# Sliding-window attention and a rational MLP on one core: from two stages to one pipeline of 256-token steps

## The chip, the cores and the metric

The kernel runs on one core of one Trainium2 chip. The metric is the device time of one execution in microseconds (us). The kernel before was run three times: 406.58, 409.15 and 409.23 us, with a median of 409.15 us.

The engines are named as in the profile: PE is TensorE (matrix products; PEld is its loading of weights), DVE is VectorE, ACT is ScalarE, POOL is GpSimd, and SP is the engine that issues most of the DMAs here. Each engine works through its own queue of instructions in the order in which it was written.

## The reference

```python
def _attn_ref(q, k, v, n_sink, window):          # q, k, v: (4, 8, 768, 64); 4 sinks, window 128
    scores = scale * np.matmul(q, k.transpose(0, 1, 3, 2))
    is_sink = pos[None, :] < int(n_sink)
    rel = pos[:, None] - pos[None, :]
    in_window = (rel >= 0) & (rel < int(window))
    scores = np.where(is_sink | in_window, scores, -1000000000.0)
    a = np.exp(scores - max); a = a / (sum(a) + 1e-09)
    return np.matmul(a, v)

x = attn_out.transpose(0, 2, 1, 3).reshape(3072, 512)
h = x @ w_in                                     # w_in (512, 2048)
P = a[0] + a[1] * h + a[2] * h**2 + a[3] * h**3
Q = 1.0 + np.abs(b[0]) * np.abs(h) + np.abs(b[1]) * h**2
out = (P / (Q + 1e-6)) @ w_out                   # w_out (2048, 512)
```

Each of 32 heads (4 batches of 8) attends over 768 positions: a position sees the 127 before it, itself, and the first four positions. The heads of a token are then put side by side, and the 3072 rows of 512 go through an MLP whose activation is a quotient of two polynomials.

## The kernel before

The kernel has two stages, one after the other. A scheduler that knows the dependences lays out each engine's queue; the order of the calls in the program is its guide.

**Attention** works on 16 pairs of heads (`for p in range(NPAIR + 5)`, L294). For each pair `load` (L181) issues six float32 loads on SP (lines 188 to 194), in runs of 64 numbers. `prepare` (L198) casts q on DVE (L202) and k on ACT into a tile with zeros between the heads (L205), and turns both by DMA (L210, L212); `prepare_v` casts v on DVE (L223). K and V stand in blocks of 64 positions; in each, one head has the upper 64 partitions and the other the lower, so that one product serves two heads. `scores` (L239) makes four products of 128x192 (L245), takes the exponential on ACT (L249) and multiplies two triangles of each block with a mask on DVE (L255). `attend` (L260) adds up to five products of 128x130 (L276), the last of them for the sinks, and divides on DVE by the sum, which stands in a 65th column (L281, L282). `emit_x` (L288) turns the result by DMA into `xT`, which holds all tokens.

**MLP** works on 24 units, 6 blocks of 512 tokens by 4 quarters of the hidden size; a unit is a tile of 128x2048 in bfloat16. `project_in` (L345) makes 32 products of 128x512 and ACT copies them out (L349). On DVE come the square (L359; every fourth unit on ACT, L357), the magnitude by a bit mask (L360), the denominator's sum (L363), the two halves of the numerator (L365, L368, L370, L371). ACT makes the reciprocal as exp(-ln) (L376, L379). The last product (L408, called the gate below) multiplies the two, and `project_out` (L387) makes 16 products of 128x512 for each 128 tokens, which ACT copies out (L390).

The call order sets how far the units overlap: the gate of a unit is called after the next unit's whole numerator and denominator (L396 to L412).

## Time and profile before

| | |
|---|---|
| median of three runs | 409.15 us (406.58 to 409.23) |
| the profiled execution's own time | 405.44 us |
| its span in the trace | 403.7 us |
| mean granted clock of PE, share of full speed | 0.871 |
| busy, share of the span | DVE 65%, PE 61%, ACT 57%, POOL 10% |
| DMA traffic | 44.36 MB, of which 41.96 MB on SP's queue (q1) and 2.14 MB on POOL's (q0) |

The span is what the trace covers; the execution's own time is 1.7 us longer. Busy shares are averages over both stages. In a page's slices the span is cut into 40 equal parts of 10.1 us, and a digit gives the tenths of a slice that something was busy. In a timeline an instruction's duration overlaps a little with the next one's start on the same engine, so what an instruction costs in a full queue is the distance from start to start.

### The profile page before, as it was taken

The page shows a single profiled execution, that of the slowest core. Times are in us where ns is not written, and L with a number is a line of the kernel's source. Part 1 is how long each engine was busy: PE and PEld are TensorE (multiplying, and loading weights), DVE is VectorE, ACT ScalarE, POOL GpSimd, SP SyncE. Part 2 cuts the span into 40 slices and gives each one's busy share as a digit, 9 for nine tenths or more (in the row PEclk, how much of TensorE's full clock was granted, in tenths as well). Part 3 has the DMA queues.
Part 4 walks back from the last instruction along what each step waited for, and adds up shares of the span by engine and source line. Part 5 has one row for each costly group of instructions (what it writes and reads, how often), then busy time and mean ns, then how long its engine had stood idle before and what let it go on. Part 6 is the DMA issues. An engine that isn't in the chain of part 4 may idle for free.

```text
span 403.7 us, 4046 instructions
## 1 busy us (share of the span) xinstructions
PE 248.1 (61%) x1403; PEld 132.8 (33%) x1424; DVE 260.8 (65%) x404; ACT 228.7 (57%) x212; POOL 40.2 (10%) x89
## 2 busy tenths in 40 slices
PE   0000015473318442744797697999999999999666
PEld 0000013253207331633552243443443443444222
DVE  0035804292207330553669999999999999999950
ACT  1002216462426232542538978978978978978741
POOL 7504970000000000000000000000000000000000
PEclk9999999595657565575899989999999999999969
DMA  8999999989999999898430001001001001001102
GB/s 253 199 222 233 189 187 193 189 146 187 189 178 157 197 184 194 150 189 168 95 59 0 2 2 52 28 27 52 28 26 52 28 26 52 28 27 53 54 26 78
DMA packets 132629, 44.36 MB, mean 110 GB/s; under 512 B 126944, under 2 KB 129024, under 8 KB 132096
## 3 DMA queue, kind: packets, MB, share of 16 engines
q1 hardware_dynamic: 129984, 41.96, 57.0%
q0 software_dynamic: 2624, 2.14, 3.2%
q8 instruction: 11, 0.18, 0.2%
...
## 4 chain that ended last, share of the span: by engine, by line
DVE 44%; DMA 16%; PE 15%; SPq 10%; issue 6%; POOL 5%; ACT 4%; POOLq 0%; DVEq 0%; ACTq 0%
DMA kT<-k_bd 7%; DVE g_t L408 6%; DVE odd L370 6%; DVE num L371 6%; PE ps_o L276 6%; PE ps_out L387 5%; DVE s_sq L359 5%; DVE num L368 4%; DVE odd L365 4%; DMA q_in<-in_q_dram 4%; SPq L210 3%; DVE den L360 3%; DVE den L363 2%; SPq L188 2%; DVE x_n L282 2%
## 5 line engine op out<-in xcount | busy, mean ns | idle before, releaser
L387 PE MATMUL ps_out<-w_out_sb,g_t 128*128 128x512 bf16 x376 | 91.7, 388 | 17.2 <-DVE g_t L408 14.4
L345 PE MATMUL ps_h<-xT,w_in_sb 128*128 128x512 bf16 x376 | 89.9, 383 | 3.9 <-ACT hb L349 3.4
L245 PE MATMUL ps<-qT,kT 128*128 128x192 bf16 x192 | 32.5, 306 | 86.1 <-DMA kT<-k_bd 77.5
L205 ACT ACTIVATE k_bd<-k_in 64x768 bf16<-64x768 f32 x32 | 26.9, 841 | 71.3 <-DMA kT<-k_bd 56.9
L376 ACT ACTIVATE lnq<-den,one_eps,qsc 128x2048 f32<-128x2048 bf16 x24 | 50.3, 2096 | 20.3 <-DVE den L363 20.2
L387 PEld LDWEIGHTS <-g_t 128*128 128x128 bf16 x384 | 37.3, 100 | 68.3 <-DVE g_t L408 24.0
L249 ACT ACTIVATE e_bd<-ps 128x768 bf16<-128x768 f32 x48 | 37.2, 809 | 39.2 <-PE ps L245 23.1
L345 PEld LDWEIGHTS <-w_in_sb 128*128 128x128 bf16 x384 | 37.7, 98 | 50.7 <-issue 8.4
L349 ACT ACTIVATE hb<-ps_h 128x1024 bf16<-128x1024 f32 x48 | 48.6, 1013 | 6.7 <-PE ps_h L345 6.7
L245 PEld LDWEIGHTS <-kT 128*128 128x128 bf16 x192 | 21.9, 122 | 90.9 <-DMA kT<-k_bd 78.7
L276 PE MATMUL ps_o<-v_bd,e_bd 128*128 128x130 bf16 x352 | 39.5, 265 | 10.4 <-DVE x_n L282 6.3
L379 ACT ACTIVATE rden<-lnq 128x2048 bf16<-128x2048 f32 x24 | 45.7, 1903 | 0.0
L202 DVE CAST q_bf<-q_in 128x768 bf16<-128x768 f32 x16 | 11.7, 728 | 49.1 <-DMA qT<-q_bf 31.8
L276 PEld LDWEIGHTS <-e_bd 128*128 128x128 bf16 x352 | 30.8, 120 | 16.7 <-DVE x_n L282 8.9
L255 DVE TENSOR_TENSOR e_bd<-e_bd,edge 128x512 bf16<-128x512 bf16 x48 | 19.2, 413 | 21.3 <-ACT e_bd L249 21.3
L408 DVE TENSOR_TENSOR g_t<-num,rden 128x2048 bf16<-128x2048 bf16 x24 | 29.4, 1226 | 0.1
L371 DVE TENSOR_TENSOR num<-num,odd 128x2048 bf16<-128x2048 bf16 x24 | 29.4, 1226 | 0.0
L370 DVE TENSOR_TENSOR odd<-odd,hb 128x2048 bf16<-128x2048 bf16 x24 | 29.4, 1226 | 0.0
L363 DVE TENSOR_TENSOR den<-den,s_sq 128x2048 bf16<-128x2048 bf16 x24 | 29.4, 1226 | 0.0
L230 PE MATMUL ps<-qT,k_sink 128*128 128x128 bf16 (+1 forms) x27 | 7.8, 404 | 30.2 <-POOL k_sink L213 30.2
L359 DVE TENSOR_TENSOR s_sq<-hb 128x2048 bf16<-128x2048 bf16 x18 | 22.1, 1226 | 3.3 <-ACT hb L349 3.3
L223 DVE CAST v_bd<-v_in 64x768 bf16<-64x768 f32 x32 | 20.0, 624 | 5.8 <-PE ps_o L276 3.9
...
## 6 DMA issues: line engine op xcount, KB each, us to landing
...
out_dram<-o_t SPq DMA_DIRECT2D x24, 256.0 KB, 2.0
...
qT<-q_bf SPq DMA_TRANSPOSE x16, 4.9
kT<-k_bd SPq DMA_TRANSPOSE x16, 3.8
```

Of the source, the lines that this page charges most:

```text
L245: nc.tensor.matmul(ps[:, n // 2, (n % 2) * 192:(n % 2) * 192 + 192], lhsT=kT[:, j, :], rhs=qT[:, 64 * j:64 * j + 192], start=True, stop=True)
L276: nc.tensor.matmul(ps_o[:, n, :], lhsT=l_, rhs=r_.rearrange("p e c -> p (e c)"), start=(m == 0), stop=(m == len(terms) - 1))
L345: nc.tensor.matmul(ps_h[:, j, :], lhsT=w_in_sb[c][:, fc * P:(fc + 1) * P], rhs=xT[c][:, t0:t0 + TB], start=(c == 0), stop=(c == NDMC - 1))
L349: nc.scalar.activation(out=hb[:, half * 2 * TB:(half + 1) * 2 * TB], in_=ps_h, func=AF.Copy)
L359: nc.vector.tensor_tensor(out=s_sq, in0=hb, in1=hb, op=ALU.mult)
L363: nc.vector.tensor_tensor(out=den, in0=den, in1=s_sq, op=ALU.add)
L370: nc.vector.tensor_tensor(out=odd, in0=odd, in1=hb, op=ALU.mult)
L371: nc.vector.tensor_tensor(out=num, in0=num, in1=odd, op=ALU.add)
L376: nc.scalar.activation(out=lnq, in_=den, func=AF.Ln, scale=qsc, bias=one_eps)
L379: nc.scalar.activation(out=rden, in_=lnq, func=AF.Exp, scale=-1.0)
L387: nc.tensor.matmul(ps_out, lhsT=g_t[:, co:co + P], rhs=w_out_sb[fc], start=(fc == 0), stop=(fc == NFFC - 1))
L408: nc.vector.tensor_tensor(out=g_t, in0=pend[2], in1=rden, op=ALU.mult)
```

## The change

Both stages become one loop over 12 steps of 256 tokens (three per batch, all eight heads). A step has two half-steps for the attention (two pairs of heads each) and two units for the MLP, each half of the hidden size (128x2048 in bfloat16, as before). In turn i of the loop the MLP works on unit i, while the attention's scores stand three half-steps and its `attend` two half-steps ahead. `project_in` now makes 32 products of 128x256 for a unit; `project_out` makes 16 of 128x512 in each turn.

- q, k and v are loaded by POOL's queue, which casts to bfloat16 on the way: a q tile of 128 tokens and all heads in one DMA, k the same, v one DMA per head and step. The casts on DVE and ACT are gone.
- K is no longer turned by DMA: eight transposes on PE for a step, and two copies from PSUM on DVE put it into the block form. q and x are turned by DMA as before, in smaller pieces.
- E and V are held by step, E in two buffers and V in three.
- In PSUM, `ps_h` has two buffers of two banks, `ps_s` one of two banks, and one pool `ps_m` of two banks serves K's transposes, the sinks, `attend` and `project_out`.
- The square is made on ACT in every second unit instead of every fourth.

```diff
@@ -30,24 +30,90 @@
...
+    TS = 256
...
+    ps_hp = ctx.enter_context(tc.tile_pool(name="ps_h", bufs=2, space=bass.MemoryType.PSUM))
+    ps_sp = ctx.enter_context(tc.tile_pool(name="ps_s", bufs=1, space=bass.MemoryType.PSUM))
+    ps_mp = ctx.enter_context(tc.tile_pool(name="ps_m", bufs=2, space=bass.MemoryType.PSUM))
...
+    def load_q(tile_i):
+        b, T = divmod(tile_i, S // P)
+        t_ = a_kv.tile([P, H, D], BF16, tag="q_bf", name="q_bf", bufs=3)
+        nc.gpsimd.dma_start(out=t_, in_=q[b, :, T * P:(T + 1) * P, :].rearrange("h p d -> p h d"))
...
+        for t in range(NTS):
+            r0 = g * TS + t * P
+            nc.gpsimd.dma_start(out=t_[:, t, :].rearrange("p (h d) -> p h d", h=H),
+                                in_=k[b, :, r0:r0 + P, :].rearrange("h p d -> p h d"))
...
+        for h in range(H):
+            i, e = divmod(h, 2)
+            nc.gpsimd.dma_start(
+                out=t_[e * 64:(e + 1) * 64, i, :, e, 0:D],
+                in_=v[b, h, g * TS:(g + 1) * TS, :].rearrange("(j p) d -> p j d", p=64))
...
-        def load(p):
...
-            q_bf = a_q.tile([P, NT, P], BF16, tag="q_bf")
-            nc.vector.tensor_copy(out=q_bf, in_=q_in.rearrange("p t e d -> p t (e d)"))
-            k_n = k_nat2[p % 2]
-            for e in range(2):
-                nc.scalar.activation(out=k_n[e * 64:(e + 1) * 64, :, e * D:(e + 1) * D],
-                                     in_=k_in[e * 64:(e + 1) * 64], func=AF.Copy)
...
-            nc.sync.dma_start_transpose(out=qT[:, 0:NT, :],
-                                        in_=q_bf.rearrange("p t c -> p (t c)"))
-            nc.sync.dma_start_transpose(out=kT, in_=k_n.rearrange("p j c -> p (j c)"))
...
-            for e in range(2):
-                nc.vector.tensor_copy(out=v_n[e * 64:(e + 1) * 64, :, e, 0:D],
-                                      in_=v_in[e * 64:(e + 1) * 64])
...
+    def turn_q(tile_i):
...
+        nc.sync.dma_start_transpose(out=qT_fix[b % 2][:, :, T * P:(T + 1) * P],
+                                    in_=q_bf.pop(tile_i).rearrange("p h d -> p (h d)"))
...
+    def turn_k(s):
+        b, g = divmod(s, GPB)
+        ps = ps_mp.tile([P, 512], FP32, tag="ps_m", name="ps_kT").bitcast(BF16)
+        ps = ps.rearrange("p (i c) -> p i c", i=NPB)
+        kb = k_bf.pop(s)
+        for t in range(NTS):
+            for i in range(NPB):
+                nc.tensor.transpose(ps[:, i, t * P:(t + 1) * P],
+                                    kb[:, t, i * P:(i + 1) * P], ident)
+        kT = kT_fix[s % 2]
+        for e in range(2):
+            lo, hi = e * 64, (e + 1) * 64
+            nc.vector.tensor_copy(out=kT[lo:hi, :, lo:hi],
+                                  in_=ps[lo:hi].rearrange("p i (j c) -> p (i j) c", c=64))
...
-        for p in range(NPAIR + 5):
...
-            if i % 4 == 3:
-                nc.scalar.activation(out=s_sq, in_=hb, func=AF.Square)
...
+        ps_h = ps_hp.tile([P, UC // 2, TS], FP32, tag="ps_h", name="ps_h")
+        for n in range(UC // 2):
+            fc = u * UC + half * (UC // 2) + n
+            for c in range(NDMC):
+                nc.tensor.matmul(ps_h[:, n, :], lhsT=w_in_sb[c][:, fc * P:(fc + 1) * P],
+                                 rhs=xblk[m][:, c, :], start=(c == 0), stop=(c == NDMC - 1))
...
+    def scores(s, i):
+        b, g = divmod(s, GPB)
+        grp, il = divmod(i, 2)
+        e_t = e_fix[grp, s % 2]
+        ps = ps_sp.tile([P, 2, 512], FP32, tag="ps_s", name="ps_s")
+        for n in range(NHF):
+            c = g * TS + 64 * n
+            nc.tensor.matmul(ps[:, n // 2, (n % 2) * 192:(n % 2) * 192 + 192],
+                             lhsT=kT_fix[s % 2][:, i * NHF + n, :],
+                             rhs=qT_fix[b % 2][:, i, c:c + 192], start=True, stop=True)
+        data = e_t[:, 64:].rearrange("p (j c) -> p j c", c=EW)[:, il * NHF:(il + 1) * NHF, 0:192]
+        nc.scalar.activation(out=data.rearrange("p (a n) c -> p a n c", a=2),
+                             in_=ps[:, :, 0:384].rearrange("p a (n c) -> p a n c", n=2),
+                             func=AF.Exp, scale=inv_sqrt_d)
+
+    def mask(s, grp):
+        e_t = e_fix[grp, s % 2]
+        blocks = e_t[:, 64:].rearrange("p (j m c) -> p j m c", m=2, c=P)[:, :, :, 0:64]
+        nc.vector.tensor_tensor(
+            out=blocks, in0=blocks,
+            in1=edge0 if s % GPB == 0 else edge.unsqueeze(1).to_broadcast([P, 2 * NHF, 2, 64]),
+            op=ALU.mult)
...
+    def attend(s, i):
+        b, g = divmod(s, GPB)
+        grp, il = divmod(i, 2)
+        ps = ps_mp.tile([P, 512], FP32, tag="ps_m", name="ps_o")
...
+            for m, (l_, r_) in enumerate(terms):
+                nc.tensor.matmul(ps_o[:, n, :], lhsT=l_, rhs=r_.rearrange("p e c -> p (e c)"),
+                                 start=(m == 0), stop=(m == len(terms) - 1))
...
+        nc.vector.reciprocal(out=rec, in_=o4[:, :, D:D + 1])
...
+    def turn_x(s, grp):
+        if grp == 0:
+            xblk[s] = xpool.tile([P, NDMC, TS], BF16, tag="xblk", name="xblk")
+        for n in range(NTS):
             nc.sync.dma_start_transpose(
...
+        if i % 2 == 0:
+            nc.scalar.activation(out=sq[i], in_=hb[i], func=AF.Square)
+        else:
+            nc.vector.tensor_tensor(out=sq[i], in0=hb[i], in1=hb[i], op=ALU.mult)
...
+    def magnitude(i):
+        den[i] = m_sb.tile([P, UW], BF16, tag="den", name="den")
+        nc.vector.tensor_scalar(out=den[i].bitcast(U32), in0=hb[i].bitcast(U32),
+                                scalar1=0x7FFF7FFF, scalar2=None, op0=ALU.bitwise_and)
+
+    def denominator(i):
+        nc.vector.tensor_tensor(out=den[i], in0=den[i], in1=sq[i], op=ALU.add)
+
+    def even(i):
+        num[i] = m_sb.tile([P, UW], BF16, tag="num", name="num")
+        nc.vector.tensor_scalar(out=num[i], in0=sq[i], scalar1=a2, scalar2=a0,
+                                op0=ALU.mult, op1=ALU.add)
+
+    def odd(i):
+        nc.vector.tensor_scalar(out=sq[i], in0=sq[i], scalar1=a3, scalar2=a1,
+                                op0=ALU.mult, op1=ALU.add)
+
+    def odd_h(i):
+        nc.vector.tensor_tensor(out=sq[i], in0=sq[i], in1=hb[i], op=ALU.mult)
+
+    def numerator(i):
+        nc.vector.tensor_tensor(out=num[i], in0=num[i], in1=sq[i], op=ALU.add)
+
+    def log_den(i):
+        lnq[i] = m_sb.tile([P, UW], FP32, tag="lnq", name="lnq", bufs=1)
+        nc.scalar.activation(out=lnq[i], in_=den[i], func=AF.Ln, scale=qsc, bias=one_eps)
+
+    def recip_den(i):
+        with nc.allow_low_precision(reason="exp(-ln(q)) reciprocal, tol 2e-2"):
+            nc.scalar.activation(out=den[i], in_=lnq[i], func=AF.Exp, scale=-1.0)
+
+    def gate(i):
+        m, u = divmod(i, 2)
+        g_of[m, u] = g_sb.tile([P, UW], BF16, tag=f"g_{u}", name=f"g_{u}")
+        nc.vector.tensor_tensor(out=g_of[m, u], in0=num[i], in1=den[i], op=ALU.mult)
+
+    def project_out(m, tt, part):
+        if part == 0:
+            ps_out[m, tt] = ps_mp.tile([P, DM], FP32, tag="ps_m", name="ps_out")
+        for fc in range(part * UC, (part + 1) * UC):
+            u, fl = divmod(fc, UC)
+            co = fl * TS + tt * P
+            nc.tensor.matmul(ps_out[m, tt], lhsT=g_of[m, u][:, co:co + P], rhs=w_out_sb[fc],
+                             start=(fc == 0), stop=(fc == NFFC - 1))
+        if part == 1:
+            o_t = o_sb.tile([P, DM], FP32, tag="o_t", name="o_t")
+            nc.scalar.activation(out=o_t, in_=ps_out[m, tt], func=AF.Copy)
+            row0 = m * TS + tt * P
...
+    load_w_in(0)
+    feed(1)
+    load_v_sink()
+    load_w_in(1)
+    load_w_out()
+    for n in range(3):
+        turn_q(n)
+    turn_k(0)
+    for i in range(-3, NU + 4):
+        s_q, grp_q = divmod(i + 3, 2)
+        s_a, grp_a = divmod(i + 2, 2)
+        has_q = s_q < NSTEP
+        has_a = 0 <= s_a < NSTEP
+        has_m = 0 <= i < NU
+        back = i - 3
+        has_o = 0 <= back < NU
+        if has_q and grp_q == 0 and s_q + 2 < NSTEP:
+            feed(s_q + 2)
+        if has_q:
+            scores(s_q, 2 * grp_q)
+        if 0 <= i - 1 < NU:
+            log_den(i - 1)
+            even(i - 1)
+            odd(i - 1)
+        if has_m:
+            project_in(i, 0)
+        if has_a:
+            attend(s_a, 2 * grp_a)
+        if 0 <= i - 1 < NU:
+            odd_h(i - 1)
+        if has_q:
+            scores(s_q, 2 * grp_q + 1)
+        if 0 <= i - 1 < NU:
+            recip_den(i - 1)
+        if has_m:
+            project_in(i, 1)
+        if has_a:
+            attend(s_a, 2 * grp_a + 1)
+            turn_x(s_a, grp_a)
+        if has_q and grp_q == 0 and 1 <= s_q + 1 < NSTEP:
+            load_v(s_q + 1)
+        if 0 <= i - 1 < NU:
+            numerator(i - 1)
+        if has_q:
+            mask(s_q, grp_q)
+        if has_m:
+            magnitude(i)
+            square(i)
+            denominator(i)
+        if has_o:
+            project_out(back // 2, back % 2, 0)
+        if has_q and grp_q == 0:
+            sink_scores(s_q)
+        if has_q and grp_q == 1 and s_q + 1 < NSTEP:
+            for n in (2 * s_q + 3, 2 * s_q + 4):
+                if n < NQT:
+                    turn_q(n)
+            turn_k(s_q + 1)
+        if 0 <= i - 1 < NU:
+            gate(i - 1)
+        if has_o:
+            project_out(back // 2, back % 2, 1)
```

What the change moves is seen in the engines' queues. First DVE in the middle of the MLP, before; `g_t` is the gate, and `den` is first the magnitude and then the denominator's sum:

```order
L359 TENSOR_TENSOR s_sq<-hb 128x2048
L360 TENSOR_SCALAR den<-hb 128x1024
L365 TENSOR_SCALAR odd<-s_sq,acoef 128x2048
L363 TENSOR_TENSOR den<-den,s_sq 128x2048
L368 TENSOR_SCALAR num<-s_sq,acoef 128x2048
L370 TENSOR_TENSOR odd<-odd,hb 128x2048
L408 TENSOR_TENSOR g_t<-num,rden 128x2048
L371 TENSOR_TENSOR num<-num,odd 128x2048
```
DVE now, in the middle of the loop, for one even unit; `kT` is K in block form, `ps_kT` its transposes, `e` the exponentials, `g` the gate:

```order
L237 COPY kT_181<-ps_kT 64x16x64 x2
L358 TENSOR_TENSOR den<-den,sq 128x2048
L362 TENSOR_SCALAR num<-sq,acoef 128x2048
L366 TENSOR_SCALAR sq<-sq,acoef 128x2048
L311 RECIPROCAL rec<-ps_o 128x4
L370 TENSOR_TENSOR sq<-sq,hb 128x2048
L313 TENSOR_TENSOR x_n<-ps_o,rec 128x2x128
L373 TENSOR_TENSOR num<-num,sq 128x2048
L311 RECIPROCAL rec<-ps_o 128x4
L281 TENSOR_TENSOR e_1_173<-e_1_173,edge 128x16x64
L313 TENSOR_TENSOR x_n<-ps_o,rec 128x2x128
L388 TENSOR_TENSOR g_2978<-num,den 128x2048
```
Before, the gate in this piece is that of the preceding unit: the sum `den<-den,s_sq` of the next unit stands ahead of it. Now the gate, the last row, follows its own unit's numerator, and the next unit's magnitude, K's copies (or a square) and sum all stand behind it; the magnitude of the unit shown is the row ahead of the first.

ACT before, for one unit and the start of the next; `lnq` and `rden` are the reciprocal's two halves, `hb` the copies of `project_in`, `o_t` the copy of `project_out`:

```order
L357 ACTIVATE s_sq<-hb 128x2048
L376 ACTIVATE lnq<-den,one_eps,qsc 128x2048
L349 ACTIVATE hb<-ps_h 128x1024
L379 ACTIVATE rden<-lnq 128x2048
L349 ACTIVATE hb<-ps_h 128x1024
L390 ACTIVATE o_t<-ps_out 128x512
```
ACT now, for the unit whose rows of DVE stand above; `den<-lnq` is the reciprocal's second half:

```order
L383 ACTIVATE den<-lnq 128x2048
L342 ACTIVATE hb<-ps_h 128x1024
L348 ACTIVATE sq<-hb 128x2048
L402 ACTIVATE o_t<-ps_out 128x512
L274 ACTIVATE e_1_173<-ps_s 128x4x192
L379 ACTIVATE lnq<-den,one_eps,qsc 128x2048
L342 ACTIVATE hb<-ps_h 128x1024
L274 ACTIVATE e_1_173<-ps_s 128x4x192
L383 ACTIVATE den<-lnq 128x2048
L342 ACTIVATE hb<-ps_h 128x1024
```
Between the two halves of the reciprocal there now stands an exponential of the attention besides the one copy of `project_in`. A second exponential stands ahead of the first half.

POOL at the start of the program, now:

```order
L72 MEMSET v_bd_92 128x2080
L72 MEMSET v_bd_96 128x2080
L74 MEMSET v_bd_92 64x16 x2
L72 MEMSET v_bd_100 128x2080
L74 MEMSET v_bd_96 64x16 x2
L80 DMA q_bf<-in_q_dram 128x8x64
L74 MEMSET v_bd_100 64x16 x2
L80 DMA q_bf<-in_q_dram 128x8x64 x2
L88 DMA k_bf<-in_k_dram 128x8x64 x2
L97 DMA v_bd_92<-in_v_dram 64x4x64 x8
masks.py:197 MEMSET ident 128x128
L117 MEMSET edge 128x128
```
Before PE can turn K it needs `ident`, which POOL fills after three fills of V's buffers and 13 loads; before, POOL's queue began with the mask and the loads of `w_out`.

## Rows read from the trace of the kernel before

**Rows 1.** The page, engines: busy us (share of the span) and instructions.
```profile
PE 248.1 (61%) x1403; PEld 132.8 (33%) x1424; DVE 260.8 (65%) x404; ACT 228.7 (57%) x212; POOL 40.2 (10%) x89
```

**Rows 2.** The page, DMA in 40 slices: mean busy share of 16 engines, in tenths.
```profile
DMA  8999999989999999898430001001001001001102
```

**Rows 3.** Stretches: length, busy us (count) PE PEld DVE ACT POOL, clock, DMA, GB/s.
```profile
100.00:120.00 20.00, 5.52 (x33) 3.92 (x32) 4.01 (x10) 5.81 (x8) 0.88 (x5) 0.59 1.18 182
220.00:240.00 20.00, 15.63 (x64) 6.46 (x64) 20.00 (x22) 18.83 (x13) 0.00 (x0) 0.91 0.00 1
340.00:360.00 20.00, 19.44 (x87) 8.49 (x88) 20.00 (x21) 19.10 (x15) 0.00 (x0) 1.00 0.07 27
```

**Rows 4.** The page, DMA queues: packets, MB, share of 16 engines' span.
```profile
q1 hardware_dynamic: 129984, 41.96, 57.0%
q0 software_dynamic: 2624, 2.14, 3.2%
```

**Rows 5.** Timeline in the MLP, VectorE and ACT: start us, us, instruction.
```profile
217.62 0.68 DVE L360 TENSOR_SCALAR den<-hb 128x1024 uint32<-128x1024 uint32 x1
218.22 0.80 DVE L365 TENSOR_SCALAR odd<-s_sq,acoef 128x2048 bf16<-128x2048 bf16 x1
218.95 1.21 DVE L363 TENSOR_TENSOR den<-den,s_sq 128x2048 bf16<-128x2048 bf16 x1
220.08 0.80 DVE L368 TENSOR_SCALAR num<-s_sq,acoef 128x2048 bf16<-128x2048 bf16 x1
220.20 2.09 ACT L376 ACTIVATE lnq<-den,one_eps,qsc 128x2048 f32<-128x2048 bf16 x1 [0.87 <-DVE den L363]
```

**Rows 6.** Groups of instructions on ACT: busy us, mean ns | idle before.
```profile
L349 ACT ACTIVATE hb<-ps_h 128x1024 bf16<-128x1024 f32 x48 | 48.6, 1013 | 6.7 <-PE ps_h L345 6.7
L379 ACT ACTIVATE rden<-lnq 128x2048 bf16<-128x2048 f32 x24 | 45.7, 1903 | 0.0
...
L249 ACT ACTIVATE e_bd<-ps 128x768 bf16<-128x768 f32 x48 | 37.2, 809 | 39.2 <-PE ps L245 23.1 <-PE ps_o L276 15.8
...
L390 ACT ACTIVATE o_t<-ps_out 128x512 f32<-128x512 f32 x24 | 14.4, 599 | 10.7 <-PE ps_out L387 10.7
```

**Rows 7.** Groups on VectorE in the attention, columns as in 6.
```profile
L255 DVE TENSOR_TENSOR e_bd<-e_bd,edge 128x512 bf16<-128x512 bf16 x48 | 19.2, 413 | 21.3 <-ACT e_bd L249 21.3
L282 DVE TENSOR_TENSOR x_n<-ps_o,rec 128x256 bf16<-128x256 f32 x48 | 19.2, 417 | 6.9 <-DMA xT<-x_n 6.4
...
L281 DVE RECIPROCAL rec<-ps_o 128x4 f32<-128x4 f32 x48 | 8.3, 176 | 4.1 <-PE ps_o L276 3.4
```

**Rows 8.** Timeline, VectorE: one cast of V.
```profile
200.40 0.56 DVE L223 CAST v_bd<-v_in 64x768 bf16<-64x768 f32 x1
```

**Rows 9.** Chain of waits, TensorE at full clock: start us, us, what, times.
```profile
204.67 1.27 PE ps_o L276 x20
...
366.24 3.45 PE ps_h L345 x16
```

**Rows 10.** Groups on POOL, columns as in 6.
```profile
L84 POOL DMA_DIRECT2D w_out_sb<-in_moe_w_out_dram x16 | 8.8, 553 | 3.9 <-DMA w_out_sb<-in_moe_w_out_dram 3.3 <-issue 0.5
...
L155 POOL MEMSET v_bd<- 128x1560 bf16 x3 | 5.0, 1680 | 0.1
L172 POOL DMA_DIRECT2D v_sink_f<-in_v_dram x8 | 4.6, 579 | 0.0
```

**Rows 11.** DMA issues: KB of each, median us from issue to landing.
```profile
out_dram<-o_t SPq DMA_DIRECT2D x24, 256.0 KB, 2.0
...
xT<-x_n SPq DMA_TRANSPOSE x16, 2.9
```

**Rows 12.** Timeline, POOL and VectorE, at 46 us.
```profile
46.08 3.10 POOL L162 MEMSET e_bd<- 128x3136 bf16 x1
...
46.55 3.03 DVE L202 CAST q_bf<-q_in 128x768 bf16<-128x768 f32 x1
```

**Rows 13.** Chain of waits, TensorE in the attention, columns as in 9.
```profile
121.99 2.02 PE ps_o L276 x17
```

450 lines of the change are left out of this document (164 added, 286 removed).

## The prediction

> **What bounds the kernel now.** The page's first part comes first: no engine is busy for more than 65% of the span [rows 1], so the span must hold stages with different limits. The slices show them: the DMA engines are 80 to 100% busy for the first 19 of 40 slices and nearly idle after [rows 2]. A table of stretches then gives each stage's limit [rows 3]. In the attention, 100 to 120 us, TensorE, VectorE and ACT are busy for 5.5, 4.0 and 5.8 of 20 us while the DMA engines are full: the transfers bound it. In the MLP, 340 to 360 us, VectorE is busy for 20.0 of 20 us, TensorE for 19.4 and ACT for 19.1. The attention with its start takes about 206 us (its last products end at 205.9 us [rows 9]), the MLP the other 198. In the transfers, q1's 129,984 packets take 57% of 16 engines' span [rows 4]: 0.57 x 403.7 x 16 / 129,984 = 28 ns each.
>
> **What goes, comes and moves.** Three costs have to be found: one turn of the new loop, the start before the first unit, and the end after the last. The attention's transfers, which bound the first stage, drop to 73,728 packets of q, k and v (18.9 MB in runs of 256 bytes) and half of the 49,152 packets of the transposes (12.6 MB, of which K with its zeros was half): at 28 ns that is 98,304 x 28 / 16 = 172 us, spread over the whole span, so no longer the bound. That casting packets cost the same no row shows. The nearest above are the 2,624 of q0, mostly of 1 KB: 0.032 x 403.7 x 16 / 2,624 = 79 ns, or 364 us for the 73,728; I take 28, because size sets most of it, and keep the other end for a rival.
>
> The turn. Its work on each engine, from start-to-start distances in the full queue [rows 5]: a two-input product or sum of 128x2048 costs VectorE 1.13 us, a polynomial's half 0.73, the magnitude 0.60.
> - VectorE: 4.5 of the first (the square only in every second unit), 2 halves, 1 magnitude, or 7.1 us; two divisions with their reciprocals, 2 x 0.59 = 1.2 [rows 7]; one mask of 128x1024, between the 0.41 of half its size and 0.83, say 0.7; K's copies, one pair in two turns. A copy of 64x1024 from PSUM is not in the trace. Below it lies the V cast, 0.56 us for 768 numbers [rows 8], or 0.75 for 1024; above it the division, which reads PSUM too: (417 - 176) / 252 = 0.96 ns per number over the reciprocal's four [rows 7], or 1.15 us. Neither row is nearer (one has the operation, the other the memory), so I take 0.95. In all 7.1 + 1.2 + 0.7 + 0.95 = 10.0 us.
> - ACT: Ln 2.09 [rows 5], Exp 1.90, two copies 2.02, two exponentials 1.62, output 0.60 [rows 6], half a square 0.95 (as Exp, which has its size), sinks about 0.2: 9.4 us.
> - TensorE at full clock: 1.27 / 20 = 64 ns for a product of 130 columns with its weights, 3.45 / 16 = 216 ns for 512 [rows 9]. So 32 of 256 at 108, 16 of 512 at 216, 18 of 130 at 64, 8 of 192 at 94, and some 6 small: 9.2 us.
>
> Three engines thus have nearly the same load, and order decides. The queues close a circle through two of them: sum on VectorE, Ln, copy, exponential and Exp on ACT, then gate, next magnitude, K's copies or square, next sum on VectorE. Before, the gate stood a half unit later and nothing waited for it. An odd unit's circle is 2.09 + 1.01 + 0.81 + 1.90 + 1.13 + 0.60 + 1.13 + 1.21 = 9.9, with two handoffs of 0.04 (sum done at 220.16, Ln at 220.20 [rows 5]) 10.0 us. In an even one the square is ACT's (1.01 + 1.90 = 2.9 us behind Exp, covered by 1.13 + 0.60 + 1.90) and K's two copies take its place: 10.75, with the bounds of the copy 10.35 to 11.15. The mean is 10.4 (10.2 to 10.6). [...] No row here shows a copy out of PSUM on VectorE.
>
> I add 0.2 for what waits at the change of step: x's last division is followed by two transposes that land 2.9 us after issue [rows 11], while TensorE has 16 x 0.216 = 3.5 us of output work and some K work as cover; with issue and queue it comes up to 1 us short in every second turn, and TensorE has slack for some of that. So 10.6 us a turn.
>
> The start. POOL fills three V buffers (1.68 us for 1560 columns [rows 10], so 2.2 each, 6.7), then issues 13 loads at 0.55 [rows 10] before `ident`: about 17 us with the small fills. K's turn and copies, then four rounds of scores and exponential in one PSUM buffer (about 1.6 us each): 27 us. But the divisions of step 0 stand on VectorE behind the eighth `w_in` cast, for which 4.2 MB of `w_in` and some 2.9 MB of loads must come: at the 182 GB/s of the attention's transfers [rows 3] 39 us, less with `w_in`'s longer rows: I take 37. Division, turning and landing: first unit at 41 us (33 if only the chain counts, 50 if `w_out` shares the transfers). Its 32 products at half clock (6.9), copy, square on ACT and sum: 11 us to the first Ln.
>
> The end. After the last Ln: 2.1 + 1.9 + gate 1.2 + 16 products 3.5 + output copy 0.6 + 2.0 to land [rows 11] = 11.3 us.
>
> **The sum.** 41 + 11 + 23 x 10.6 - 3 (the last turns have no exponentials and no K) + 11.3 = 304 us of span, against 403.7. The profiled execution took 1.7 us more than its span, 405.44, and the median of the runs 409.15 is 0.9% above it: 304 + 1.7 = 306, and 308 for a median. The casts on VectorE and ACT that go are counted for nothing of their own: they lay under the transfers [rows 2]. What is late next is VectorE, at 10.0 of 10.6 us.
>
> **Rivals.**
> - The circle has slack I don't see and transfers start sooner: VectorE's work alone, 9.7 with a quick copy, from 33 us: 33 + 11 + 223 - 3 + 11 = 275, a median of 280. For it: before, VectorE never waited in the MLP [rows 3]. Against: the order of the rows.
> - POOL's issues get in VectorE's way. A cast that takes about 0.56 us alone took 3.03 beside a POOL fill of 3.10 us [rows 12, 8]. In the MLP before, POOL did nothing [rows 3]; now it issues six loads a turn. If each of the three single-input operations of a unit met one issue of 0.55 [rows 10], a turn would be 10.4 + 1.7 = 12.1 us and the median 343. Against: rows of an issue beside VectorE there are none; in the fills POOL writes 128 partitions all the time. [...] Other small waits (two `ps_m` buffers for four uses) would end in the same place.
> - The loads bound. An issue of 128 rows takes 0.55 us, one of 16 rows 0.58 [rows 10], so rows seem free; a q or k tile has 1,024 runs. If they were not, 8 x 0.55 = 4.4 for 48 tiles, 1.1 for 96 V loads and 20 for the rest make 337 us of issuing, with five turns behind the last 390, a median of 395. It decides from 21 us of issuing per step, which two turns hide. With 79 ns a packet it ends near there too.
> [...]
>
> That the stages might not overlap is excluded: the queues interleave them.
>
> **Chances.** The forecast 0.57, the quick case 0.12, VectorE's waits 0.20, the loads 0.04, the clock 0.05, nothing that can be told 0.02. About 1% is what a measurement of this kernel can tell. Faster by over 1%: 0.93; within 1%: 0.02; slower: 0.05. The range reaches into the quick case (start at 33 us alone gives 300, with 9.8 a turn 281) and past the third (343): 282 to 352. Left out are the loads, the clock and the outer halves of the two others.
>
> **What would show it.** First `ps_h` product near 41 us; gates of successive units 10.0 and 10.75 us apart in turn; VectorE waiting up to a microsecond for ACT ahead of each gate, and nowhere else; a kT copy near 0.95 us; TensorE at full clock from there on; POOL's issues under 1 us for 1,024 runs. Wrong would be: gates 12 us or more apart, single-input operations of VectorE longer than before, TensorE waiting for x or `ps_m` longer than 1 us a turn, K's or Q's tiles late.

## The result, and the profile after

The changed kernel takes 320.06 us (median of 4 runs, 318.43 to 320.73) against 408.33 us (the kernel before, now with a fourth run): a ratio of 0.784, 95% interval 0.779 to 0.788. The profiled execution has a span of 318.6 us. The forecast was 308, from a sum of 304 us of span, so the sum was 14.6 us short, and its terms missed by more than that, in both directions.

First the page of the changed kernel: its engines, the granted clock and the DMA engines in 40 slices, and the two DMA queues (packets, MB, share of 16 engines).

```profile
PE 240.5 (75%) x1920; PEld 167.4 (53%) x1920; DVE 250.4 (79%) x384; ACT 212.8 (67%) x194; POOL 127.1 (40%) x192
...
PEclk9999556979858998999999999999999999999999
DMA  4999999999999996996960627549510111110011
...
q0 software_dynamic: 78976, 11.56, 58.1%
q1 hardware_dynamic: 31776, 16.79, 23.6%
```

Before, the busiest engine had 65% of the span [rows 1] and the DMA engines were full for the first half and idle in the second [rows 2]. Now VectorE has 79%. The transfers did not spread over the span, though: the DMA engines are full from 8 to about 120 us, thin out up to 225 us, where the last load is issued, and are then nearly idle. A packet of q0 took 0.581 x 318.6 x 16 / 78,976 = 37.5 ns, where the forecast took 28 and had 79 as its other end. (The DMA share adds up the times of all packets and can pass 1, as the 1.60 from 48 to 112 us in the next table does.)

The table of stretches of the changed kernel, as [rows 3] before (us, busy us of each engine and its instructions, granted clock, DMA share, GB/s):

```profile
48.00:112.00 64.00, 45.50 (x372) 33.46 (x372) 41.61 (x67) 38.50 (x34) 45.85 (x63) 0.82 1.60 118
112.00:225.00 113.00, 101.30 (x857) 71.04 (x855) 105.52 (x156) 95.24 (x88) 44.32 (x63) 0.98 0.76 77
225.00:300.00 75.00, 69.34 (x563) 48.48 (x562) 68.74 (x93) 63.26 (x57) 0.00 (x0) 1.00 0.15 42
```

From 48 to 112 us, with the transfers full, TensorE, VectorE and ACT are busy for 71, 65 and 60% of the time. From 112 us on they have 90, 93 and 84%. So the new pipeline has a slow first third and an even rest. Where one ends is read from ACT's Ln, one for each of the 24 units. The rows are ACT's timeline (start, duration, what; behind it in brackets the idle time ahead of it and what ended it):

```profile
61.12 2.09 ACT L379 ACTIVATE lnq<-den,one_eps,qsc 128x2048 f32<-128x2048 bf16 x1
...
104.91 2.09 ACT L379 ACTIVATE lnq<-den,one_eps,qsc 128x2048 f32<-128x2048 bf16 x1
...
208.76 2.10 ACT L379 ACTIVATE lnq<-den,one_eps,qsc 128x2048 f32<-128x2048 bf16 x1 [1.01 <-DVE den L358]
...
278.34 2.10 ACT L379 ACTIVATE lnq<-den,one_eps,qsc 128x2048 f32<-128x2048 bf16 x1 [0.81 <-DVE den L358]
...
305.56 2.10 ACT L379 ACTIVATE lnq<-den,one_eps,qsc 128x2048 f32<-128x2048 bf16 x1 [0.99 <-DVE den L358]
```

They are the 1st, 4th, 14th, 21st and 24th Ln, and they give the sum term by term:

| term | forecast | measured |
|---|---|---|
| up to the first Ln | 52 us | 61.1 us |
| the first 13 turns | 138 us (10.6 each) | 147.6 us (11.4 each) |
| the next 7 turns | 74 us (10.6 each) | 69.6 us (9.94 each) |
| the last 3 turns | 29 us | 27.2 us |
| from the last Ln to the end | 11.3 us | 13.0 us |

At the even pace of 9.94 us the first 13 turns would take 129.2 us. They took 18.4 us more, and the start 9.1 us more than its term. The even turn gave back 0.66 us 23 times, 15.2 us. Of the 18.4 us, 14.0 lie in the first three turns (43.8 us up to the fourth Ln instead of 29.8). Two questions are left: what sets the even turn, and what slows the start and the turns up to 208 us.

**The even turn.** This is the chain of waits of the changed kernel over one even unit (start, duration, what). Each piece begins as the one before it ends; pieces of 0.03 us and less are left out:

```profile
208.76 2.10 ACT lnq L379
210.86 0.90 ACT hb L342
211.77 0.70 ACT e L274
212.47 1.81 ACT den L383
...
214.30 1.23 DVE g L388
215.53 0.61 DVE den L354
216.13 0.06 DVE kT L237
216.19 0.54 issue
216.74 0.69 DVE kT L237
...
217.46 1.23 DVE den L358
```

It is the circle of the forecast, piece by piece: Ln, copy, exponential, Exp, gate, magnitude, K's two copies, sum, and the next Ln at 218.74. It takes 9.98 us, not 10.75. Through the odd unit that follows the chain stays on VectorE:

```profile
218.98 0.72 DVE num L362
...
219.73 0.89 DVE sq L366
...
220.84 1.11 DVE sq L370
...
222.29 1.13 DVE num L373
...
224.42 1.13 DVE g L388
225.56 0.60 DVE den L354
226.16 1.13 DVE sq L350
...
227.36 1.20 DVE den L358
```

There the gate does not wait for ACT at all. The stretch of these two units, in the columns of the table of stretches, has VectorE busy for 19.44 of 19.89 us and TensorE for 18.60:

```profile
208.76:228.65 19.89, 18.60 (x164) 13.20 (x163) 19.44 (x33) 17.40 (x17) 12.04 (x18) 1.00 0.84 78
```

So in the chain the circle and VectorE's own work bind in turn, with almost the same length, and TensorE's work is not far below.

**The slow turns.** The 20.5 us between the third and the fourth Ln are the worst. In SyncE's queue (the timeline, in order of issue) and VectorE's (below it) at that place stand:

```profile
82.17 2.84 SPq L222 DMA_TRANSPOSE qT<-q_bf  x2
85.11 2.53 SPq L324 DMA_TRANSPOSE xblk<-x_n  x2
92.43 4.32 SPq L222 DMA_TRANSPOSE qT<-q_bf  x2
96.85 2.49 SPq L324 DMA_TRANSPOSE xblk<-x_n  x2
```

```profile
79.25 0.42 DVE L313 TENSOR_TENSOR x_n<-ps_o,rec 128x256 bf16<-128x256 f32 x1
```

x's last division for the first half of the third step ends at 79.7 us. Its transposes are issued 5.4 us later, because ahead of them in the queue stand two transposes of Q: tiles 11 and 12 counted from 0, the fourth pair since 55 us, for the sixth and the seventh step. They could not be issued before their tiles had landed, and the tiles came late: between 76 and 100 us SyncE's queue waited 16.9 us for tiles of Q. The second half fared no better: its division ends at 89.6 us, and its transposes go at 96.85, behind the next pair of Q's. Then x itself was slow to land, as the chain of waits shows:

```profile
86.41 5.75 DMA xblk<-x_n
...
92.20 1.03 PE ps_h L339 x4
...
98.10 4.10 DMA xblk<-x_n
...
102.25 1.72 PE ps_h L339 x14
```

After 5.75 us for the one half and 4.10 for the other, TensorE can go on at 102.25 us. In the chain from 140 us on the same landing takes 2.33 to 2.40. In the list of waits this is the largest wait of TensorE (us in total, times, longest):

```profile
PE ps_h L339 <- DMA xblk<-x_n: 30.6, 14, 8.9
```

### The profile page after: what moved, and what is told of

Its sections match the earlier page's. It is cut to its first block, busy times and chain, and to the rows that moved or that the text cites. A ratio compares the mean times of both kernels' runs of the same rounds, so it can differ in the third digit from the quotient of the medians.

```text
span 318.6 us, 5033 instructions
## 1 busy us (share of the span) xinstructions
PE 240.5 (75%) x1920; PEld 167.4 (53%) x1920; DVE 250.4 (79%) x384; ACT 212.8 (67%) x194; POOL 127.1 (40%) x192
## 3 DMA queue, kind: packets, MB, share of 16 engines
q0 software_dynamic: 78976, 11.56, 58.1%
## 4 chain that ended last, share of the span: by engine, by line
DVE 33%; ACT 21%; DMA 19%; PE 10%; issue 7%; POOL 5%; SPq 3%; DVEq 0%; ACTq 0%; POOLq 0%
DMA xblk<-x_n 12%; ACT lnq L379 7%; ACT den L383 6%; DVE den L358 5%; DVE g L388 5%; PE ps_h L339 5%; DVE num L373 4%; DVE sq L370 4%; PE ps_out L398 3%; ACT e L274 3%; SPq L324 3%; DVE den L354 3%; ACT hb L342 3%; DVE num L362 2%; DMA q_bf<-in_q_dram 2%
## 5 line engine op out<-in xcount | busy, mean ns | idle before, releaser
L339 PE MATMUL ps_h<-xblk,w_in_sb 128*128 128x256 bf16 x768 | 98.0, 278 | 30.7 <-DMA xblk<-x_n 30.6
L339 PEld LDWEIGHTS <-w_in_sb 128*128 128x128 bf16 x768 | 74.4, 100 | 45.6 <-DMA xblk<-x_n 28.1
L398 PE MATMUL ps_out<-w_out_sb,g 128*128 128x512 bf16 x384 | 93.5, 391 | 3.7 <-DVE g L388 3.4
L97 POOL DMA_DIRECT2D v_bd<-in_v_dram x96 | 61.8, 663 | 55.4 <-PE ps_o L305 47.3
L274 ACT ACTIVATE e<-ps_s 128x768 bf16<-128x768 f32 x48 | 38.7, 806 | 53.2 <-PE ps_s L270 53.2
L398 PEld LDWEIGHTS <-g 128*128 128x128 bf16 x384 | 37.3, 101 | 44.0 <-issue 5.1
L383 ACT ACTIVATE den<-lnq 128x2048 bf16<-128x2048 f32 x24 | 45.8, 1908 | 0.0
L305 PE MATMUL ps_o<-v_bd,e 128*128 128x130 bf16 x352 | 31.4, 226 | 3.0 <-DMA v_bd<-in_v_dram 1.8
L388 DVE TENSOR_TENSOR g<-num,den 128x2048 bf16<-128x2048 bf16 x24 | 29.4, 1223 | 5.4 <-ACT den L383 5.3
L358 DVE TENSOR_TENSOR den<-den,sq 128x2048 bf16<-128x2048 bf16 x24 | 29.4, 1223 | 2.5 <-ACT sq L348 2.0
L281 DVE TENSOR_TENSOR e<-e,edge 128x1024 bf16<-128x1024 bf16 x24 | 16.2, 675 | 17.7 <-ACT e L274 17.7
```

What stands on the lines that cost most here:

```text
L97: nc.gpsimd.dma_start(out=t_[e * 64:(e + 1) * 64, i, :, e, 0:D], in_=v[b, h, g * TS:(g + 1) * TS, :].rearrange("(j p) d -> p j d", p=64))
L274: nc.scalar.activation(out=data.rearrange("p (a n) c -> p a n c", a=2), in_=ps[:, :, 0:384].rearrange("p a (n c) -> p a n c", n=2), func=A ...
L305: nc.tensor.matmul(ps_o[:, n, :], lhsT=l_, rhs=r_.rearrange("p e c -> p (e c)"), start=(m == 0), stop=(m == len(terms) - 1))
L339: nc.tensor.matmul(ps_h[:, n, :], lhsT=w_in_sb[c][:, fc * P:(fc + 1) * P], rhs=xblk[m][:, c, :], start=(c == 0), stop=(c == NDMC - 1))
L358: nc.vector.tensor_tensor(out=den[i], in0=den[i], in1=sq[i], op=ALU.add)
L383: nc.scalar.activation(out=den[i], in_=lnq[i], func=AF.Exp, scale=-1.0)
```

## The experiments

The theory that the first of them tested: the early turns are long because the loads fill the DMA engines, and the even turn is bound by the circle and by VectorE's work together. All ratios are to the kernel before; the changed kernel's is 0.784 (0.779 to 0.788).

| run | ratio, 95% interval | span | first, fourth, 14th Ln |
|---|---|---|---|
| the changed kernel | 0.784 (0.779 to 0.788) | 318.6 | 61.1, 104.9, 208.8 |
| later loads left out | 0.780 (0.776 to 0.784) | 316.3 | 69.6, 102.6, 205.2 |
| mask left out | 0.775 (0.771 to 0.780) | 316.5 | 61.4, 105.4, 205.3 |
| gate a turn later | 0.783 (0.779 to 0.787) | 317.2 | 60.4, 100.6, 205.0 |
| both of these | 0.771 (0.768 to 0.774) | 315.7 | 61.0, 105.8, 205.5 |
| w_out later | 0.796 (0.793 to 0.798) | 322.9 | 63.3, 110.1, 213.1 |
| sinks' V first (time alone) | 0.790 (0.787 to 0.793) | - | - |
| start by need | 0.788 (0.784 to 0.792) | 317.8 | 57.5, 103.9, 205.8 |
| the same, one K buffer | 0.785 (0.783 to 0.787) | 317.6 | 56.7, 97.2, 206.4 |
| Q behind x | 0.763 (0.758 to 0.768) | 310.6 | 59.5, 96.8, 197.9 |
| start by need, Q behind x | 0.775 (0.772 to 0.777) | 312.2 | 56.6, 96.7, 199.8 |
| Q behind x, one transpose for a half of x | 0.747 (0.742 to 0.752) | 305.5 | 62.3, 97.9, 195.5 |
| 15 of w_out's 16 loads left out | 0.779 (0.773 to 0.785) | 313.2 | 62.0, 99.8, 201.2 |

**Later loads left out.** For K from the third step on, and likewise for Q and V:

```diff
     def load_k(s):
+        if s >= 2:
+            k_bf[s] = k_all[s % 2]
+            return
```

> This kernel leaves out the loads of q, k and v after the first steps (K of steps 2 and up, Q's tiles from the fifth, V from the fourth step): the later steps use the numbers of the first ones again. Everything else stays. Theory: the turns between the first Ln at 61 us and the one at 169 us of the changed kernel (12.0 us each on average against 9.9 later) are long because the loads run ahead and keep the DMA engines full until about 112 us, so that x's transposes land 5 to 7 us after issue instead of 2.3. Then the first Ln comes a few us sooner at most (w_out still shares the transfers), the turns after it take 10 us from about the third on, and the span falls by 15 to 19 us, from 318.6 to 300 to 304. Rival: the early turns are long because the pipeline fills (attention two steps ahead on the same engines, TensorE at half clock): then they stay long and the span is 315 or more. Second rival, POOL's issues slow VectorE: then the turns between 125 and 225 us would also fall, by up to 1.7 us each.

The 13 turns behind the first Ln took 205.2 - 69.6 = 135.6 us instead of 147.6. Of these 12.0 us, 10.8 lie in the first three turns, which also began 8.5 us later; the ten behind them took 102.6 us instead of 103.9. So it is not shown how much of the 12.0 the loads had cost and how much the later start gave, and the 14th Ln came only 3.6 us sooner. The even pace stayed: 9.94 us from the 14th to the 21st Ln, though POOL had nothing left to issue after 61 us (225 in the changed kernel), so POOL's issues do not lengthen the even turn. The time itself fell by only 2 us, which is not clear of the changed kernel's interval, since the first Ln came 8.5 us later. The expectation did not have that, and SyncE's queue of this run shows it:

```profile
39.35 8.83 SPq L231 DMA_TRANSPOSE qT<-q_bf  x4
48.27 3.35 SPq L333 DMA_TRANSPOSE xblk<-x_n  x2
```

The division of the first step's second half of x ended at 42.6 us, but its transposes were issued only at 48.27 (41.49 in the changed kernel), because four transposes of Q stood ahead of them; the first unit's products went on at 58.48 us instead of 49.58.

**The even turn: the mask left out, the gate a turn later, both.** (issue_after(x) queues what stands in its block behind x on x's engine.)

```diff
-        if has_q:
+        if has_q and s_q == 0:
             mask(s_q, grp_q)
```

```diff
-        if 0 <= i - 1 < NU:
-            gate(i - 1)
...
+        if 0 <= i - 2 < NU:
+            with tc.issue_after(odd_ins[i - 1].ins):
+                gate(i - 2)
```

> This kernel leaves out the mask of the band's edges after the first step: 22 operations of VectorE of 0.68 us that stand in no step of the circle sum, Ln, copy, exponential, Exp, gate, magnitude, square or K's copies, sum. Theory: the circle (9.8 us in an odd unit, 9.97 in an even one by the durations of the changed kernel) and VectorE's work (9.7 of 9.9 us) bound the turn together, so it gives almost nothing: the turns stay between 9.7 and 9.9 us and the span falls by 0 to 4 us. Rival, VectorE's work alone is the bound: the turn falls by 0.6 us and the span by 14, to 305.

> The gate of a unit is issued one turn later, behind the next unit's two polynomial halves, and so no longer between Exp and the next magnitude: the circle loses the gate and Exp, and VectorE's work stays as it is. Theory (both bounds together): VectorE's work alone is left, 9.7 us, and the turn falls by 0 to 0.3 us, the span by 0 to 7. Rival, the circle alone is the bound: with slack in VectorE the turn falls by more, to 9.3 us (TensorE's and ACT's work), the span by 14. Rival on the other side: the products that need the late gate come later, TensorE waits for them, and it is slower by some us.

> Both edits at once: the gate a turn later, and the mask left out after the first step. Theory (the circle and VectorE's work bound the turn together): only the two together shorten it, to the work of the engine that is next, TensorE with 9.3 us; the span falls by 10 to 16 us, more than the sum of the two single edits. If one of them alone was the bound, this run equals the run with that edit.

From the 14th to the 21st Ln the turn is 9.94 us in the changed kernel, 9.89 without the mask, 10.06 with the late gate, and 9.78 with both. That neither single edit moves it by more than 0.12 us fits two bounds of one length: 0.68 us less of VectorE's work are worth nothing while the circle stands, and opening the circle is worth nothing while VectorE has 9.7 us to do. The third expectation failed: both together gave 0.16 us a turn, and 1.6% of the time by the ratios, or 5 us, not 10 to 16. The next bound was nearer than I had put it. In four turns of that run (the columns as above)

```profile
195.89:235.00 39.11, 36.99 (x324) 26.73 (x323) 36.45 (x56) 35.23 (x33) 14.17 (x22) 1.00 0.65 70
```

TensorE is busy for 36.99 of 39.11 us, 9.25 a turn and 95%. With its short waits for x and for output products it fills the turn. Three engines within 5% of each other leave little to a single edit. That TensorE is the bound there is not shown: no run took work from it. The single edits are not quite without effect either: by the ratios the mask alone gave 1.1%, the two intervals just touching at 0.779 to 0.780. The profiled executions of the mask's run and of the run with both were the slowest of theirs (318.19 us with a median of 315.49, and 317.40 with 314.59), so their turns may show too little.

**The start: four orders of the same loads, and one load left out.** w_out's loads behind the V of the third step:

```diff
-    load_w_out()
...
+        if i == 0:
+            load_w_out()
```

> Only the issue of w_out's 16 loads moves in POOL's queue: from ahead of the second step's remaining loads to behind the V loads of the second and third step. In the changed kernel they were issued from 32 to 46 us; their 2,048 packets took 112 ns each, 14 us of all 16 engines, x's second transposes of step 0 landed 8 us after issue, and the second step's V came behind them. Theory (transfers set the start): the first Ln comes 4 to 8 us sooner (at 53 to 57 us instead of 61); some of it may be given back by longer turns behind it, where w_out's transfers now lie; span 311 to 318. Rival (the start is set by TensorE's order and its clock): the first Ln stays at 60 us or more and the span at 318. On the other side: the first output products wait for w_out and the turns at 80 to 100 us get longer than what the start gained.

The sinks' V ahead of the second step's loads:

```diff
+    load_v_sink()
     feed(1)
-    load_v_sink()
```

> Only the eight small loads of the sinks' V move in POOL's queue, from behind the second step's K and Q tiles to ahead of them. In the changed kernel step 0's last attention products waited 4.5 us for them, and the chain of the end runs through them (the Q tile's load 7.2 us, the sinks' load 2.6 us, then the first division at 34.2 us). Theory: the first division comes 5 us sooner, near 29 us; but x's first transposes would then meet the casts and loads of w_in (the second half lands behind 36 us) so that the first products come 2 to 4 us sooner, near 41, and the span falls by 0 to 4 us. Rival (the first unit waits for w_in or for w_out's transfers anyway): the first Ln stays at 61.

Both, and K's and Q's first loads and the matrix for K's turn ahead of the fills of the V buffers, which now stand where the "..." is:

```diff
+    load_k(0)
     for n in range(3):
         load_q(n)
-    load_k(0)
-    load_v(0)
     ident = const_pool.tile([P, P], BF16, name="ident")
     make_identity(nc, ident)
...
+    load_v(0)
```

> The start in the order in which things are needed, with the same loads: K's and Q's first loads ahead of the fills of the V buffers on POOL, the small matrix for K's turn next, the sinks' V ahead of the second step's loads, w_out behind the V of the third step. Theory (the DMA engines set the start: up to the first Ln they have to move w_in with 1,024 packets of about 200 ns, 13 us, and 8,000 to 10,000 packets of 35 ns, 20 us, and stood half idle for the first 8 us): first K turn near 13 us instead of 18.9, first Ln at 48 to 53 us instead of 61, span 305 to 312. Rival: the start is set elsewhere and the first Ln stays within 3 us of the one in the run with w_out alone late.

The same with one K buffer, and a step's K and Q issued behind K's turn of the step before:

```diff
-        t_ = a_kv.tile([P, NTS, H * D], BF16, tag="k_bf", name="k_bf")
+        t_ = a_kv.tile([P, NTS, H * D], BF16, tag="k_bf", name="k_bf", bufs=1)
...
-        if has_q and grp_q == 0 and s_q + 2 < NSTEP:
-            feed(s_q + 2)
...
             turn_k(s_q + 1)
+            if s_q + 2 < NSTEP:
+                feed(s_q + 2)
```

> The start of the run before it (first loads, sinks, w_out), and the loads run less far ahead: one K buffer instead of two, and a step's K and Q loads are issued only once the K of the step before it is turned. Theory (running ahead fills the DMA engines until about 112 us and makes x's transposes late): the turns up to 169 us, which took 1.5 to 2 us more than the later ones on average, lose up to half of that, 5 to 8 us less in all than in the run before it; span 298 to 306. Rival: the step's own loads (6,144 packets of 35 ns, 13.4 us of all 16 engines, in a step of 20) are what x's transposes meet, wherever they lie: no gain, the same span. On the other side: K comes late, and every step waits for it, slower than the run before it by 10 us or more.

The first two cost time: 0.796 and 0.790, both above the changed kernel's interval, the second by little (0.787 to 0.793). The third brought the first Ln 3.6 us forward, less than expected, and the fourth Ln only 1.0 us; the fourth kernel reached its fourth Ln 7.7 us sooner and had lost all but 2.4 us of it by the 14th. Both missed their expected spans, 305 to 312 and 298 to 306, with 317.8 and 317.6. In the run with w_out later the wait moved to another tile: the chain runs through a Q tile that took 10.56 us to land and then held back x's transposes:

```profile
34.68 10.56 DMA q_bf<-in_q_dram
45.26 1.23 SPq L222
46.58 1.19 SPq L324
47.81 6.00 DMA xblk<-x_n
53.86 2.85 PE ps_h L339 x14
```

The division of x's second half had ended at 41.7 us, 4.9 us before these transposes of x.

It is that row of SyncE's queue, Q's transpose ahead of x's, that led to the next theory. The last run asked it from the other side, by leaving transfers out:

```diff
-        for c in range(NFFC):
+        for c in range(1):
             nc.gpsimd.dma_start(out=w_out_sb[c], in_=moe_w_out[c * P:(c + 1) * P, :])
...
-    w_out_sb = [wpool.tile([P, DM], BF16, name=f"w_out_sb_{c}") for c in range(NFFC)]
+    w_out_sb = [wpool.tile([P, DM], BF16, name=f"w_out_sb_{c}") for c in range(1)] * NFFC
```

> The changed kernel with 15 of w_out's 16 loads left out (all sixteen blocks of the output product use the first one): 1,920 packets of 113 ns less, 13.6 us of all 16 engines between 32 and 55 us; nothing else changes place. It asks what the start, forecast at 52 us up to the first Ln and measured at 61.1, is made of. Theory (w_out's transfers share the engines with x's first transposes, which then took 7 to 8 us to land, and hold back the second step's V): the first Ln at 52 to 57 us, the fourth 5 to 12 us sooner than 104.9, span 308 to 314. Rival (moving w_out later gained nothing, so what comes next in POOL's queue takes its place at once): the first Ln at 59 us or later; what the fourth Ln gains then shows whether the sum of the transfers counts behind it. On the other side nothing speaks for more than 319.

The rival was right: the first Ln stayed, at 62.0 us. The K and Q loads behind w_out took the freed engines at once (a DMA share of 1.63 from 20 to 50 us, against 1.24 in the changed kernel), and Q's transposes got ahead of x's second half, divided by 41.6 us, in SyncE's queue:

```profile
43.50 3.24 SPq L222 DMA_TRANSPOSE qT<-q_bf  x2
46.83 2.48 SPq L324 DMA_TRANSPOSE xblk<-x_n  x2
```

The fourth Ln came 5.2 us sooner, which fits that the sum of the transfers counts behind the start; the time, 0.779 (0.773 to 0.785), is not clear of the changed kernel's.

**Q's transposes behind x's.** Only SyncE's order changes; since a Q buffer comes free at its turn, Q's loads are paced too:

```diff
+                if s_q > 0:
+                    st.enter_context(tc.issue_after(x_ins[s_q - 1, 1].ins))
                 for n in (2 * s_q + 3, 2 * s_q + 4):
                     if n < NQT:
                         turn_q(n)
```

> Only the order on SyncE's queue changes: the transposes of Q's next two tiles are issued behind x's transposes of the turn before, and no longer up to two steps ahead of them. In the changed kernel tiles 11 and 12 (for the sixth step) were turned at 82 us, ahead of x's transposes for the third step, whose divisions were done at 79.6 us and which were issued at 85.1 us, since the queue stood at Q tiles that had not landed. Theory A (the queue's order): the third step's x comes 5 us sooner, the long turn behind it (20.5 us, 84.4 to 104.9) loses 5 to 8 us, and Q's loads run less far ahead too, since a Q buffer comes free at its turn; the fourth Ln near 97 us, span 308 to 313. Theory B (the transfers' sum): what has to be moved up to there is the same, x's transposes still take 5 to 7 us to land, the fourth Ln stays between 103 and 107 us and the span at 316 to 320. On the other side: scores wait for a Q tile that is now turned too late, and turns of 10 us get longer all along, span above 325.

> Both: the start in the order of need (K and Q ahead of the fills, the sinks' V early, w_out behind the third step's V), and Q's transposes behind x's of the turn before. Alone, the start brought the first Ln from 61.1 to 57.5 us, and the fourth from 104.9 only to 103.9. Theory A (the queue's order ate what the start had gained): the fourth Ln near 93 us, span 304 to 309. Theory B (the transfers' sum): the fourth Ln at 101 us or later, span 315 or more.

Theory A held, in size too. In SyncE's queue of the first of the two

```profile
68.07 2.55 SPq L222 DMA_TRANSPOSE qT<-q_bf  x2
79.54 13.15 SPq L324 DMA_TRANSPOSE xblk<-x_n  x4
```

the third step's x is issued at 79.54 us, as soon as its division is done (85.11 in the changed kernel), its second half at 90.23 (96.85), and the fourth Ln is at 96.8 us. The first 13 turns take 197.9 - 59.5 = 138.3 us instead of 147.6, and the ratio of 0.763 lies clear of the changed kernel's. Not all of it need be the order. The two halves of the third step's x also landed sooner after their issue, in 3.5 and 3.0 us where the changed kernel had 6.0 and 4.2, and Q's loads were paced too; no run separates the two. K's and Q's loads paced without the order, in the run with one K buffer, gave nothing that is clear (0.785 after 0.788). With the start by need on top, the expectation failed: the fourth Ln stayed at 96.7 us (93 was expected), and it ended later than without it. The gain of that start is lost again by the fourth Ln, whatever SyncE's order.

**One transpose for a half of x.** x's tiles are laid out so that one transpose of 128x512 does what two of 128x256 did:

```diff
-        for n in range(NTS):
-            x_ins[s, grp] = nc.sync.dma_start_transpose(
-                out=xblk[s][:, 2 * grp:2 * grp + 2, n * P:(n + 1) * P],
-                in_=x_n[s][:, n, grp * 2 * P:(grp + 1) * 2 * P])
+        x_ins[s, grp] = nc.sync.dma_start_transpose(
+            out=xblk[s][:, grp].rearrange("p n c t -> p (n c) t"),
+            in_=x_n[s][:, grp].rearrange("p n c -> p (n c)"))
```

> On top of the order of Q's transposes behind x's: each half of x is turned by one transpose of 128x512 instead of two of 128x256 (x's two tiles are laid out side by side for it). In the changed kernel one of the two took 1.2 us of SyncE's queue and landed 2.3 us after issue, so that the last half of x reached TensorE 4.8 us after its division, where the forecast had 2.9; TensorE waited for x 22 us in all in the run before it, and the turns came in pairs of 20.3 to 21.4 us up to the eleventh, 19.9 behind it. Theory (x's way to TensorE at the change of step is what is left): 1.2 us less at each change of step at which TensorE waits, the pairs fall to 19.9 to 20.3, the span falls by 4 to 10 us to 301 to 307. Rival (the transfer's length, not its issue, is what counts: a transpose of twice the size lands later by what the issue saves): no change, 308 to 312. Second rival: VectorE's and ACT's circle takes what x gives back: pairs fall by less than 0.3, span 307 to 310.

The theory held: 305.86 us, ratio 0.747, faster than both kernels. The rows are x's transposes in the answer on x's tile (duration in ns min/median/max, first and last start), without this edit and with it:

```profile
L324 SPq DMA_TRANSPOSE xblk<-x_n x48: 1168/1229/2553, 34.5 to 273.5; - x48
...
  DMA xblk<-x_n: 22.0, 13
```

```profile
L323 SPq DMA_TRANSPOSE xblk<-x_n x24: 1189/1190/1613, 34.9 to 269.7; - x24
...
  DMA xblk<-x_n: 11.4, 6
```

A transpose of twice the size occupies SyncE's queue as long as one of half the size, 1.2 us, and its median landing is 2.5 us, against 2.4. TensorE's wait for x fell from 30.6 us in the changed kernel to 22.0 and then to 11.4, and the first 13 turns from 147.6 to 138.3 and to 133.2 us. Of the 18.4 us above the even pace, 9.3 thus went with the order of Q's and x's transposes, 5.1 with the double issue, and 4.0 are left. Part of the 5.1 is a first Ln that came 2.8 us later; the 14th came 2.4 us sooner.

## Why the prediction was right, and where its sum was not

- **What bounds the new loop** held. After the early turns the circle of the forecast stands in the chain, and VectorE's work is as long as the circle. The rival without a circle (VectorE's work alone, a turn of 9.7) named the other of the two bounds. Which of the two binds changes from unit to unit. The experiments fit that and do not prove it: neither alone could be removed with much profit, and both together gave so little that TensorE's work, 18.60 of 19.89 us, may be a third bound of nearly the same length.
- **The turn's size** was off by 0.66 us. Of it 0.2 is what I had added for the change of step; the rest is the circle, 9.98 us in the even unit above (10.75 forecast) and 9.91 in the odd one (10.0). The largest part in the even unit is K's copy: 0.69 us (0.667 to 0.695) against the 0.95 taken between the bounds 0.75 and 1.15, so it lay below both. Two copies in an even unit make 0.52 us. The 0.95 was my estimate between a cast and a division, neither of them a copy out of PSUM; the 24 copies of this trace are the first that show one. The 9.7 of the rival without a circle has a quick copy that no row of before shows; with the 0.69 measured, VectorE's work comes to 9.7. The other 0.3 us come from ACT: copy, exponential and Exp take 0.90 + 0.70 + 1.81 in the chain, where I had added their durations, 1.01 + 0.81 + 1.90 [rows 6]. The durations of these instructions, which follow without a gap, overlap by 0.1 us; I had used start-to-start distances for VectorE and not for ACT.
- **Gates 10.0 and 10.75 us apart in turn** did not show: from 204 to 244 us the gates are 9.84 to 10.04 apart. VectorE's wait ahead of the gate is at most 1.1 us, as told, and at 13 of the 24 gates; but it also waited elsewhere, 17.7 us in all for exponentials ahead of the mask.
- **"I add 0.2 for what waits at the change of step"** is the step that failed in the turns. It counted the landing of 2.9 us [rows 11] and neither SyncE's queue nor a busy transfer. The way of x is two issues of 1.2 us, behind each other and behind Q's transposes, and a landing of 2.3 us, or 4 to 7 while the loads run: 30.6 us of TensorE's waits in all, 14.5 of them between the first and the fourth Ln, instead of some 5. I wrote that a tile's lateness would show me wrong, but had not followed what stands behind a late tile in its queue. In the even turns the cover by output products nearly holds: three waits of up to 1.1 us in seven turns, 2.7 us in all.
- **"No longer the bound, spread over the whole span"** failed with it. A casting packet took 37.5 ns, near the end that I chose, but the loads run ahead as far as the buffers let them, up to three steps, so the DMA engines are full for 110 us and the demand that should have been spread comes first. The landings of x fit that: 2.3 us once POOL's queue is thin, 5.75 and 4.10 in the chain while it is full. How the engines divide their time between the two queues is not shown.
- **The start** was 9.1 us short: the first products came at 44.3 us (41 was forecast), and then the first unit took 16.8 us instead of 11, since x's second half landed 8 us after its issue and the second step's V held up VectorE's queue. My upper bound of 50 had w_out sharing the transfers, and it does. But of the kernels that move or remove loads at the start none brings the fourth Ln below 96.7 us. A start that moves only what the first unit needs was not tried, so what bounds it stays open; what is shown is that the DMA engines are at least 90% busy in every slice from 8 to 64 us in the changed kernel, with w_out later and with w_out once, so that neither moving w_out's loads nor leaving them out made room there. In three of these runs (later loads left out, w_out later, w_out once) x's second half stood 4.9 to 5.7 us behind Q's transposes in SyncE's queue, so they do not show what less traffic alone would give. TensorE's clock may have a part too: in the changed kernel 0.50 was granted from 40 to 48 us and 0.64 from 48 to 56, over most of the first unit's wait and products, after TensorE had been busy for 3.7 us from 32 to 40; in the run with w_out once 1.00 was granted from 20 to 50 us, with 2.9 us busy from 32 to 40. The two differ in x's arrival too, so no run shows what the clock costs.
- **The end**: 13.0 us for 11.3; the output landed 3.3 us after its copy, not 2.0.
- **The rivals.** POOL in VectorE's way: the three single-input operations of a unit take 0.13 us more while POOL issues than after it, not 1.7. The rows are of one of them, the magnitude, in the two stretches (busy us, operations; 0.78 and 0.69 us each); the polynomial's halves take 0.02 us more each:

```profile
120.00:225.00 105.00, 7.84 (x10) 0.99 0.72 73
225.00:300.00 75.00, 5.51 (x8) 1.00 0.15 42
```

  The loads as bound: POOL's issue of 1,024 runs took 0.90 us, not 4.4, so the queue of issues never bound; the transfers made x and Q's tiles late, most of it in the first third of the span. The clock, which had 0.05 of the chances: granted 0.82 of full speed between 48 and 112 us and 0.98 to 1.00 behind it (with TensorE busy 71% and 90 to 92%), and 0.936 over the span (0.871 before), so a lower clock did not set the even turn.

The total came out 4% off by luck, better than its terms, because a turn that was too long by 0.66 us 23 times hid a start and an early stretch that were too short by 27 us.
